# The second MoE product of three token groups as seven block products, in a kernel of linear attention followed by a MoE block

## The chip, the cores and the metric

The kernel runs on one core of a Trainium2 chip. The metric is the time of one execution on the device in microseconds (us). Five engines work side by side, each with its own queue of instructions that it takes in order: PE (TensorE, matrix products; the profile lists its weight loads apart, as PEld), DVE (VectorE), ACT (ScalarE), POOL (GpSimd) and SP, which here only issues DMAs. They wait for one another through semaphores.

## The reference

```python
def _attn_ref(q, k, v, w_phi):          # q, k, v: 8 batches, 8 heads, 576 tokens, 64 wide
    def phi(x):
        proj = np.einsum('bhsd,df->bhsf', x, w_phi)                 # 128 features
        proj = proj - np.max(np.abs(proj), axis=-1, keepdims=True)
        return np.concatenate([np.exp(proj), np.exp(-proj)], axis=-1)
    q_p, k_p = (phi(q), phi(k))
    kv = np.einsum('bhsf,bhsd->bhfd', k_p, v)
    z = np.sum(k_p, axis=2)
    num = np.einsum('bhsf,bhfd->bhsd', q_p, kv)
    den = np.einsum('bhsf,bhf->bhs', q_p, z)[..., None] + 1e-06
    return (num / den).astype(np.float32)

def _moe_ref(x, g_ln, w_ch1, w_ch2):    # x: 8 x 576 tokens, 512 wide; w_ch1 512 x 2048, w_ch2 2048 x 512
    mu = np.mean(x, axis=-1, keepdims=True)
    var = np.mean((x - mu) ** 2, axis=-1, keepdims=True)
    xn = (x - mu) / np.sqrt(var + 1e-06) * g_ln
    ch = np.maximum(xn @ w_ch1, 0.0) @ w_ch2
    return (x + ch).astype(np.float32)
```

The output of the attention, with the heads side by side, is the input x of the MoE block. Inputs and output are fp32.

## The kernel before

The eight batches are taken as four pairs. The attention of a pair is done in eight units of two heads each (32 units in all). A unit transposes its q and k (on PE in the first units, by DMA later), projects them (`pm`, `pt`), takes maxima on DVE and exponentials on ACT, scales v on POOL (`vv`), forms the kv product in two halves (`n_bank`, L945 and L951), and the numerator (`num`, L1013 and L1019). DVE scales and adds the numerator (`numc`) and POOL divides it and writes the rows of x (L1057). Nine tiles of 128 tokens belong to a pair: eight whole ones, and a mixed one that holds the last 64 tokens of both batches; half of its rows is moved between partitions by a DMA (L976).

The MoE block works on groups of NM = 4 tiles, 512 tokens: eight groups of whole tiles, numbered by pair and batch, and one group MIX of the four mixed tiles. In `moe`, a group's first product (`first`, L1246) makes 16 blocks of hidden units, each with 4 matmuls of 512 columns, and ACT or DVE apply the ReLU and write hT in bf16. The second product (`second`, L1312) makes each token tile with 16 matmuls of 512 columns; ACT or DVE scale it by the tile's 1/std, POOL or DVE add x, and SP stores it (L1221 for a whole tile; L1230, two DMAs of 64 rows, for a mixed one). The second product of a group is issued among the first products of the next one. The order of the last three groups is 6, then MIX = 7, then 8 = LAST, which holds the last four whole tiles of pair 3. The last tile of group 8 is made by `half` (L1278) in two halves of 256 columns, and DVE adds and scales in one instruction (L1286).

The order in which every engine gets its instructions is made by a planner (`Order`) ahead of the run. `add` records an operation with its engine or engines, an assumed duration, the keys that it reads and writes, and its rank; PSUM tiles are counted by `acquire` and `release`. The rank of an attention operation is its latest start plus an offset from the table OFF, by the unit's row (`stage_table`) and the kind of operation. Where PE would have nothing to do in the first 75 us of the plan, dummy products of 120 columns are put in (L1512). The DMAs of loads, of transposes and of stores go through SP's queue in the planned order.

Of the kernel before, what the change touches and what calls it, by code (L numbers as in the profile page):

```python
# [10 lines left out]
FP32 = mybir.dt.float32  # L11
# [6 lines left out]
def bcast(ap: bass.AP, dim: int, n: int) -> bass.AP:  # L18
# [7 lines left out]
RELU = -983.1  # L26
# [11 lines left out]
        "load": 291.2, "trans": -38.2, "trans.copy": 0.5, "mixed": 98.0, "mixed.max": 104.5,  # L38
        "mixed.exp": -45.3, "mixed.fold": 0.0, "k": -23.0, "k.max": 3.0, "k.em": -170.0,
        "k.exp": 48.6, "en": -19.6, "vv": 80.6, "q": -83.6, "q.max": 0.0, "q.em": -32.0,  # L40
        "tails": 0.0, "tails.exp": -33.1, "kv": -2.6, "kv.copy": 164.7, "num0": -1.6,
        "num1": -20.8, "num.dve": -35.2, "g1": 0.0, "g2": 0.0, "g3": 0.0, "put": 3.5,
# [3 lines left out]
        "load": 291.2, "trans": 67.9, "trans.copy": 77.3, "mixed": 113.2, "mixed.max": 2.5,  # L46
        "mixed.exp": 213.3, "mixed.fold": 0.0, "k": -107.2, "k.max": -82.3, "k.em": 0.0,
        "k.exp": 6.2, "en": 473.7, "vv": -103.0, "q": -117.1, "q.max": 22.6, "q.em": -113.8,
        "tails": 0.0, "tails.exp": 165.0, "kv": -37.9, "kv.copy": -50.3, "num0": 37.2,
        "num1": -11.3, "num.dve": -149.4, "g1": 0.0, "g2": 0.0, "g3": 0.0, "put": -83.2,  # L50
        "ln": -11.9, "w1": -144.2, "w2": -136.8, "ln.c": -23.8, "ln.t": -23.8,
    },
    {
        "load": 291.2, "trans": 1.5, "trans.copy": -233.5, "mixed": -82.7, "mixed.max": 122.1,
        "mixed.exp": -1.1, "mixed.fold": 0.0, "k": 0.0, "k.max": -8.9, "k.em": -29.8,
        "k.exp": 0.0, "en": 7.8, "vv": 31.7, "q": 171.9, "q.max": 0.0, "q.em": 0.0,
        "tails": -7.0, "tails.exp": 17.2, "kv": 3.1, "kv.copy": 23.8, "num0": 0.2,
        "num1": 234.6, "num.dve": 11.4, "g1": 0.0, "g2": 0.0, "g3": 0.0, "put": -23.6,
        "ln": -23.8, "w1": -144.2, "w2": 29.5, "ln.c": -23.8, "ln.t": -23.8,
    },  # L60
    {
        "load": 291.2, "trans": 88.5, "trans.copy": 90.6, "mixed": 98.6, "mixed.max": -74.3,
        "mixed.exp": -98.9, "mixed.fold": 0.0, "k": 57.3, "k.max": -34.9, "k.em": 25.5,
# [3 lines left out]
        "w2": -136.8, "ln.c": 37.5, "ln.t": 0.0,  # L67
    },
    {
        "load": 0.5, "trans": -177.0, "trans.copy": 128.5, "mixed": -1.4, "mixed.max": -3.9,  # L70
        "mixed.exp": 16.5, "mixed.fold": 0.0, "k": -79.5, "k.max": -16.8, "k.em": -20.4,
        "k.exp": -42.2, "en": -14.1, "vv": -42.3, "q": 271.6, "q.max": -32.6, "q.em": 5.9,
        "tails": -412.8, "tails.exp": -63.8, "kv": 72.7, "kv.copy": 39.3, "num0": 0.0,
        "num1": 70.0, "num.dve": -0.3, "g1": 41.9, "g2": -13.9, "g3": -5.0, "put": -25.6,
# [234 lines left out]
def kernel(  # L309
# [43 lines left out]
    NB16 = 3  # L353
# [769 lines left out]
    def token_tile(g, i):  # L1123

        pair, t = (i, MX) if g == MIX else (g // NR, g % NR * NM + i)
        if g > MIX:
            pair, t = NPAIR - 1, MX - NM + i
# [220 lines left out]
    def moe(g):  # L1348
# [3 lines left out]
        for jj in range(JC):  # L1352
            if g <= LAST:
                first(g, jj)
# [197 lines left out]
```

## Time and profile before

| | us |
|---|---|
| median of 3 runs (377.04 to 377.27) | 377.05 |
| the profiled execution, its own time | 375.46 |
| its span, first to last instruction | 373.7 |

| busy in the span | us |
|---|---|
| first products on PE (L1246, 576 matmuls) | 137.3 |
| second products on PE (L1312, 560 matmuls) | 132.5 |
| ReLU on ACT (L1256, 93 instructions) | 55.6 |
| ReLU on DVE (L1254, 51 instructions) | 35.0 |
| addition of x on POOL (L1329, 18 of the whole tiles) | 21.1 |
| last tile's result on DVE (L1286, 2 halves) | 1.0 |

The profile counts matmuls as overlapping: the shown duration of one of 512 columns, 379 ns, is its time through the pipeline, and the next one starts sooner. How fast a row of products goes is therefore read from the chain of waits or the timeline, as duration of a piece divided by its count. Busy shares are those of the engine, not of the critical path.

### The profile page before, as it was taken

The page shows a single profiled execution, that of the slowest core. Times are in us where ns is not written, and L with a number is a line of the kernel's source. Part 1 is how long each engine was busy: PE and PEld are TensorE (multiplying, and loading weights), DVE is VectorE, ACT ScalarE, POOL GpSimd, SP SyncE. Part 2 cuts the span into 40 slices and gives each one's busy share as a digit, 9 for nine tenths or more (in the row PEclk, how much of TensorE's full clock was granted, in tenths as well). Part 3 has the DMA queues.
Part 4 walks back from the last instruction along what each step waited for, and adds up shares of the span by engine and source line. Part 5 has one row for each costly group of instructions (what it writes and reads, how often), then busy time and mean ns, then how long its engine had stood idle before and what let it go on. Part 6 is the DMA issues. An engine that isn't in the chain of part 4 may idle for free.

```text
span 373.7 us, 9165 instructions
## 1 busy us (share of the span) xinstructions
PE 358.2 (96%) x3490; PEld 204.4 (55%) x3490; DVE 244.2 (65%) x517; ACT 271.0 (73%) x564; POOL 216.3 (58%) x441
## 2 busy tenths in 40 slices
PE   8968898998999999999999999999999999999995
PEld 8856784554454545555545554555455544444444
DVE  4859898986889968876797689777957740000001
ACT  4866998796979897878997899688958663643520
POOL 4597998674945867576757675775566523001211
PEclk9999999999999999999999999999999999999999
DMA  8999999989996795486539242913040043002112
GB/s 211 286 216 232 187 261 252 234 214 237 265 225 177 174 236 164 104 185 211 125 119 203 102 91 58 209 59 66 25 93 36 26 89 119 22 0 56 44 42 84
DMA packets 92587, 53.61 MB, mean 143 GB/s; under 512 B 58992, under 2 KB 87984, under 8 KB 92544
## 3 DMA queue, kind: packets, MB, share of 16 engines
q1 hardware_dynamic: 87504, 47.99, 51.1%
q0 software_dynamic: 4416, 4.49, 7.2%
q10 hardware_dynamic: 624, 0.56, 0.5%
q8 instruction: 27, 0.44, 0.5%
q14 instruction: 16, 0.13, 0.1%
HBM read 36.77 MB, written 9.44 MB: 124 GB/s over the span
## 4 chain that ended last, share of the span: by engine, by line
PE 75%; DMA 14%; DVE 7%; POOL 1%; issue 1%; SPq 0%; DVEq 0%; POOLq 0%
PE ch_ps L1312 29%; PE hT_ps L1246 29%; DMA qk<-in_q_dram 8%; DMA qkT<-b 4%; PE pm L796 3%; PE n_bank L951 3%; PE num L1013 3%; DVE m L853 2%; PE pt L805 2%; DMA qx<-in_k_dram 2%; PE n_bank L1512 1%; PE ch_ps L1278 1%; PE n_bank L945 1%; DVE numc L1037 1%; DVE hT L1254 1%
## 5 line engine op out<-in xcount | busy, mean ns | idle before, releaser
L1246 PE MATMUL hT_ps<-xT,w 128*128 128x512 bf16 x576 | 137.3, 379 | 0.5 <-DVE hT L1254 0.4
L1312 PE MATMUL ch_ps<-w,hT 128*128 128x512 bf16 x560 | 132.5, 379 | 0.0
L853 DVE TENSOR_REDUCE m<-pm 128x8 f32<-128x1024 f32 x64 | 76.7, 1215 | 11.7 <-PE pm L796 9.6
L1246 PEld LDWEIGHTS <-w 128*128 128x128 bf16 x576 | 52.1, 98 | 56.2 <-issue 2.8
L1312 PEld LDWEIGHTS <-hT 128*128 128x128 bf16 x560 | 51.6, 98 | 55.2
L1256 ACT ACTIVATE hT<-hT_ps 128x512 bf16<-128x512 f32 x93 | 55.6, 598 | 30.8 <-PE hT_ps L1246 29.4
L921 ACT ACTIVATE ea<-pt 128x1024 bf16<-128x1024 f32 x64 | 63.6, 1034 | 7.5 <-PE pt L805 7.2
L867 ACT ACTIVATE eb<-pm 128x1024 bf16<-128x1024 f32 x64 | 64.2, 1033 | 2.7 <-DVE m L853 2.7
L1057 POOL TENSOR_TENSOR x<-numc,rden 128x64 bf16<-128x64 f32 (+1 forms) x128 | 48.4, 401 | 20.8 <-DVE rden L1049 19.2
L879 POOL TENSOR_TENSOR vv<-v,em 128x512 bf16<-128x512 f32 x32 | 33.5, 1047 | 45.0 <-ACT em L858 29.3
L1286 DVE SCALAR_TENSOR_TENSOR o<-ch_ps,rstd,x 128x256 f32<-128x256 f32 x2 | 1.0, 484 | 65.8 <-PE ch_ps L1278 65.8
L1254 DVE TENSOR_SCALAR hT<-hT_ps 128x512 bf16<-128x512 f32 x51 | 35.0, 687 | 12.1 <-PE hT_ps L1246 11.7
L1329 POOL TENSOR_TENSOR o<-o,x 128x512 f32<-128x512 f32 x18 | 21.1, 1173 | 31.6 <-ACT o L1325 31.3
L1325 ACT ACTIVATE o<-ch_ps,rstd 128x512 f32<-128x512 f32 x22 | 15.1, 687 | 28.2 <-PE ch_ps L1312 28.2
L879 POOL TENSOR_TENSOR vv<-v,en 128x512 bf16<-128x512 f32 x32 | 33.4, 1043 | 1.9 <-ACT en L872 1.8
L1013 PEld LDWEIGHTS <-ea 128*128 128x128 bf16 x512 | 23.9, 97 | 10.3 <-issue 1.6
L1512 PE MATMUL n_bank<-wz 128*128 128x120 bf16 x393 | 28.4, 222 | 0.6 <-ACT KV L961 0.5
L951 PE MATMUL n_bank<-vv,eb 128*128 128x65 bf16 x512 | 26.9, 194 | 0.0
L951 PEld LDWEIGHTS <-eb 128*128 128x128 bf16 x512 | 22.3, 98 | 5.7 <-issue 1.4
L1512 PEld LDWEIGHTS <-wz 128*128 128x128 bf16 x393 | 23.9, 101 | 2.1 <-issue 1.2
L1037 DVE TENSOR_TENSOR numc<-num,em 128x390 f32<-128x390 f32 (+1 forms) x40 | 20.4, 516 | 4.3 <-PE num L1013 4.2
L1329 POOL TENSOR_TENSOR o<-o,xm 128x512 f32<-128x512 f32 x4 | 4.6, 1153 | 31.7 <-ACT o L1325 31.7
(99 smaller groups left out, 508.4 us busy)
## 6 DMA issues: line engine op xcount, KB each, us to landing
out_dram<-o SPq DMA_DIRECT2D x31, 256.0 KB, 2.8
qk<-in_k_dram SPq DMA_DIRECT2D x12, 512.0 KB, 5.8
qk<-in_q_dram SPq DMA_DIRECT2D x12, 512.0 KB, 6.9
v<-in_v_dram SPq DMA_DIRECT2D x12, 512.0 KB, 5.2
w<-in_moe_w_ch_dram POOLq DMA_DIRECT2D x8, 512.0 KB, 11.1
qk<-in_k_dram SPq DMA_DIRECT2D x8, 256.0 KB, 6.9
qk<-in_q_dram SPq DMA_DIRECT2D x7, 256.0 KB, 7.6
v<-in_v_dram SPq DMA_DIRECT2D x7, 256.0 KB, 7.9
```

What stands on the lines that cost most here:

```text
L853: nc.vector.reduce_max(out=m, in_=ps, axis=AX.X, apply_absolute_value=True)
L867: nc.scalar.activation(eb, ps, AF.Exp, scale=(1.0, -1.0)[t])
L879: nc.gpsimd.tensor_tensor(out=u["vv"][:, t, 0:MX, 0:D], in0=vb[:, hh, :].rearrange("p (c d) -> p c d", d=D), in1=bcast(e[:, 0:MX], 2, D), ...
L921: nc.scalar.activation(u["EA"][:, t, 0:1024], u["pt"], AF.Exp, scale=(1.0, -1.0)[t])
L951: nc.tensor.matmul(ps[:, t, c // 4, :], EB[:, t, c, :], vv[:, t, c, :], start=False, stop=(t == 0 and c == MX - 1), skip_group_check=True,)
L1013: nc.tensor.matmul(ps[t][:, i, :], ea(u, t, c), KV[:, t, c // 4, :], start=True, stop=True,)
L1057: nc.gpsimd.tensor_tensor(out=dst, in0=st["numc"][ps_, i : i + n, 0:D], in1=bcast(st["rden"][ps_, i : i + n], 2, D), op=ALU.mult,)
L1246: nc.tensor.matmul(st["ps"], w1_sb[:, kc, jj * P : (jj + 1) * P], xT_bufs[g % XB][:, kc::KC, :], start=(kc == 0), stop=(kc == KC - 1),)
L1254: nc.vector.tensor_relu(h_sb, st["ps"])
L1256: nc.scalar.activation(h_sb, st["ps"], AF.Relu)
L1312: nc.tensor.matmul(ch[g, i], hT[g, jj][:, i * P : (i + 1) * P], w2_sb[:, jj, :], start=(jj == 0), stop=(jj == JC - 1),)
L1512: nc.tensor.matmul(warm, wz, wz[:, 0:WN], start=False, stop=False, skip_group_check=True)
```

## The change

The last three groups (`FAST`) get another second product. For two token tiles A1 and A2 (the rows of hT, its 16 blocks of hidden units split into even and odd ones) and for w2 (rows split in the same way, columns into two halves of 256) the product is a 2 x 2 product of blocks. It is made by Strassen's scheme in Winograd's form, with seven block products instead of eight: each is 8 matmuls of 256 columns, on blocks, on four sums S of blocks of hT, or on four sums T of blocks of w2. Two pairs of tiles make up a group, so there are 14 steps of 8 matmuls; the first two products of each pair are split in halves of 4 matmuls. Three accumulators of 256 columns (`chain`) are used for a pair, and each product's partial sum is added to the output tile by DVE as it stands, seven results per pair; so a chain goes on only when the result before it has been read.

The four sums T are formed once (`weight_sums`, 8 instructions on DVE or POOL), the four sums S for each group (`token_sums`, 16 instructions on DVE, half of them after the ninth first product, half after the last). They lie in the buffers of q, k and v that the attention no longer uses. hT becomes one ring of 24 fixed slots.

The group of the mixed tiles becomes the last one (MIX = LAST = 8), and groups 6 and 7 are the whole tiles of pair 3. In the last group the second pair is stored in halves of 256 columns, each in two DMAs of 64 rows. `half` is gone. The table OFF has other numbers and one more row, for the units of pair 3.

```diff
-        "load": 291.2, "trans": -38.2, "trans.copy": 0.5, "mixed": 98.0, "mixed.max": 104.5,
+        "load": 291.2, "trans": -41.8, "trans.copy": 16.1, "mixed": -153.8, "mixed.max": 92.2,
...
-    MIX = LAST - 1
+    MIX = LAST
+    FAST = (LAST - 2, LAST - 1, LAST)
+    CP = JC // 2
+    FH = DM // 2
+    SH = CP // 2
...
+    ring = consts.tile([P, HB, RN], BF16, name="hT")
+    wide = [t.bitcast(BF16).rearrange("p a u f -> p (a u f)") for t in qk_bufs]
+    small = [t.bitcast(BF16).rearrange("p u f -> p (u f)") for t in v_bufs]
...
+    def weight_sums():
+        B11, B12 = w2_sb[:, 0::2, 0:FH], w2_sb[:, 0::2, FH:DM]
+        B21, B22 = w2_sb[:, 1::2, 0:FH], w2_sb[:, 1::2, FH:DM]
+        T1, T2, T3, T4 = T_of
+        todo = ((T1, B12, B11, ()), (T2, B22, T1, (0,)), (T3, B22, B12, ()), (T4, B21, T2, (1,)))
...
+                add(("DVE", "POOL"), (Port(0.6), 2.0), (), emit,
...
+    def token_sums(g, c):
+        for p in range(NM // 2):
...
+                out_, a, b, op = (
+                    (S1, blocks(1, 0), blocks(1, 1), ALU.add),
+                    (S2, S1, blocks(0, 0), ALU.subtract),
+                    (S3, blocks(0, 0), blocks(1, 0), ALU.subtract),
+                    (S4, blocks(0, 1), S2, ALU.subtract),
+                )[i]
+                nc.vector.tensor_tensor(out=out_, in0=a, in1=b, op=op)
...
+    def fast(g, p, i, cs):
...
+        left, right, chain, t, f, s_key, t_key = (
+            (A(t0, 0), B(0, f1), 0, t0, f1, None, None),
+            (A(t0, 1), B(1, f1), 1, t0, f1, None, None),
+            (S(1), T(1), 0, t0, f2, 1, 1),
+            (S(0), T(0), 2, t1, f2, 0, 0),
+            (S(2), T(2), 0, t1, f2, 2, 2),
+            (S(3), B(1, f2), 2, t0, f2, 3, None),
+            (A(t1, 1), T(3), 0, t1, f1, None, 3),
+        )[i]
...
+            nc.vector.scalar_tensor_tensor(
+                out=o, in0=ch[g, p][:, bank, cols : cols + FH], scalar=rstd_x[:, g, t : t + 1],
+                in1=token_tile(g, t)[2][:, f] if fresh else o, op0=ALU.mult, op1=ALU.add,
+            )
...
+        if g == LAST and p == NM // 2 - 1:
+            if not fresh or i == 6:
+                dma("SP", counts["V"], 131072, lambda: store(g, t, ch["o", g, t], f.start, f.stop),
+                    r=o_key)
...
     def moe(g):
         done = 0
+        if g == FAST[0]:
+            weight_sums()
         for jj in range(JC):
             if g <= LAST:
                 first(g, jj)
+            if g - 1 in FAST:
+                pairs_, h1, h2 = range(NM // 2), range(SH), range(SH, CP)
+                steps = [(p, i, cs) for cs in (h1, h2) for p in pairs_ for i in range(2)]
+                steps += [(p, i, range(CP)) for i in range(2, 7) for p in pairs_]
+                until = min(len(steps), -(-(jj + 1) * len(steps) // 8))
+                for step in steps[done:until]:
+                    fast(g - 1, *step)
+                done = until
+            if g in FAST and jj in (SH * 2, JC - 1):
+                token_sums(g, 0 if jj < JC - 1 else SH)
...
     def stage_table(n):
-        return min(n, H) + (n >= 2 * H)
+        return min(n, H) + (n >= 2 * H) + (n >= 3 * H)
...
-                groups = (*[g for g in groups if g < MIX], MIX, LAST)
+                groups = (*groups, MIX)
```

Over the whole program PE gets 336 matmuls of 256 columns (`fast`, L1421 of the changed file) for 176 of 512 and 32 of 256, and 402 dummy products for 393. Three places show how the change moves instructions. L numbers in the rows of the change are lines of the changed file, where everything behind the table stands lower.

The first is the end of DVE's program, in the last group. Before, DVE has nothing there but the statistics of the mixed tiles, long ahead, and the last tile's two results:

```order
L1186 BN_AGGR mv<-st 128x2
L1174 BN_STATS st<-xm 128x6
L1186 BN_AGGR mv<-st 128x2
L1191 TENSOR_SCALAR xc_137<-xm,mv 128x512
L1286 SCALAR_TENSOR_TENSOR o<-ch_ps,rstd,x 128x256 x2
```

Now the sums S of the second half of the hidden units stand there (L1375, into the old buffers qk_100, v_103 and v_105), and among them the results (L1430) of the two pairs (ch_6062 and ch_6072):

```order
L1375 TENSOR_TENSOR qk_100<-hT 128x512
L1375 TENSOR_TENSOR v_103<-hT 128x512
L1375 TENSOR_TENSOR qk_100<-qk_100,hT 128x512
L1375 TENSOR_TENSOR v_103<-v_103,hT 128x512
L1375 TENSOR_TENSOR qk_100<-hT 128x512
L1430 SCALAR_TENSOR_TENSOR o<-ch_6062,rstd,xm 128x256
L1375 TENSOR_TENSOR v_105<-hT 128x512
L1430 SCALAR_TENSOR_TENSOR o<-ch_6062,rstd,o 128x256
L1430 SCALAR_TENSOR_TENSOR o<-ch_6072,rstd,xm 128x256
L1375 TENSOR_TENSOR qk_100<-hT,qk_100 128x512
```

Five sums stand ahead of the first pair's first result, one more sum and one result ahead of the second pair's.

The second place is the end of SP's queue, with the stores of the last two groups. Before:

```order
L1221 DMA out_dram<-o 128x512 x4
L1230 DMA out_dram<-o 64x512 x8
L1221 DMA out_dram<-o 128x512 x3
L1221 DMA out_dram<-o 128x256 x2
```

And now:

```order
L1231 DMA out_dram<-o 128x512 x8
L1240 DMA out_dram<-o 64x256 x4
L1240 DMA out_dram<-o 64x512 x2
L1240 DMA out_dram<-o 64x256 x2
L1240 DMA out_dram<-o 64x512 x2
L1240 DMA out_dram<-o 64x256 x2
```

The last four tiles took five DMAs of 128 rows; they take twelve of 64 rows, of which the last ten belong to the last five pairs of DMAs.

The third place is POOL's queue in the ramp, about units 2 to 5, where POOL writes the rows of x (L1057, in the changed file L1069; `x` whole tiles, `xs` and `xm` the mixed one) and scales v (`vv`). Before, the rows of unit 3 (the rows of x in the last `128x64 x2` and the two `128x3x64`) stand behind the v of unit 4 and partly of unit 5:

```order
L1057 TENSOR_TENSOR x<-numc,rden 128x64
L1057 TENSOR_TENSOR xs<-numc,rden 64x64
L1057 TENSOR_TENSOR xm<-numc,rden 64x64
L1057 TENSOR_TENSOR x<-numc,rden 128x64 x2
L1057 TENSOR_TENSOR xs<-numc,rden 64x64
L1057 TENSOR_TENSOR x<-numc,rden 128x3x64
L879 TENSOR_TENSOR vv<-v_105,em 128x8x64
L884 CAST vv<-em 128x8
L888 TENSOR_TENSOR vv<-vx_107,em 128x130
L1057 TENSOR_TENSOR x<-numc,rden 128x3x64
```

And now:

```order
L1069 TENSOR_TENSOR x<-numc,rden 128x3x64
L588 DMA w_132<-in_moe_w_ch_dram 128x4x512
L1069 TENSOR_TENSOR x<-numc,rden 128x3x64 x3
L891 TENSOR_TENSOR vv<-v_105,em 128x8x64
L896 CAST vv<-em 128x8
L900 TENSOR_TENSOR vv<-vx_107,em 128x130
L1069 TENSOR_TENSOR x<-numc,rden 128x64 x2
L891 TENSOR_TENSOR vv<-v_105,em 128x8x64
```

Unit 3's rows of whole tiles, the last that group 0 needs, now stand ahead of unit 5's v and of three of the four halves of the v of units 4 and 5; the mixed rows `xs` and `xm` of units 2 and 3 follow behind them. On PE the transposes of group 0's tokens (L1138) stand behind nine halves of kv products where they stood behind twelve.

More of the change, by code (lines that the diff above doesn't have):

```diff
@@ new lines @@
+    {
+        "load": 7.2, "trans": 138.6, "trans.copy": 96.2, "mixed": 359.4, "mixed.max": 9.3,
+        "mixed.exp": 4.2, "mixed.fold": 0.0, "k": -33.5, "k.max": -1.4, "k.em": -15.1,
+        "k.exp": 3.5, "en": -6.3, "vv": -77.6, "q": -27.3, "q.max": -738.0, "q.em": 8.0,
+        "tails": -210.6, "tails.exp": -25.8, "kv": -17.8, "kv.copy": -18.3, "num0": 53.8,
+        "num1": 47.3, "num.dve": -78.8, "g1": 4.1, "g2": -68.2, "g3": -93.8, "put": 0.0,
+        "ln": 104.9, "w1": 193.2, "w2": 28.2, "ln.c": 8.6, "ln.t": -5.8,
@@ L1362, in moe @@
                 done += n
-        if g > LAST:
-            for c0 in range(0, DM, DM // 2):
-                for j0 in range(0, JC, 4):
-                    half(LAST, NM - 1, c0, j0, 4)
     def stage_table(n):
-        return min(n, H) + (n >= 2 * H)
+        return min(n, H) + (n >= 2 * H) + (n >= 3 * H)
     def rk(stage, n):
```

230 lines of the change are left out of this document (140 added, 90 removed), and 10 rows, old and new, of the table OFF.

## The prediction

> **What bounds the kernel now.** I read the page's first two parts, then the waits of TensorE (PE) from 100 us on, then a table by stage, then the chain that ended last.
>
> ```profile
> span 373.7 us, 9165 instructions
> PE 358.2 (96%) x3490; PEld 204.4 (55%) x3490; DVE 244.2 (65%) x517; ACT 271.0 (73%) x564; POOL 216.3 (58%) x441
> ```
> ```profile
> engine line waited for: us in total, times, longest us
> PE num L1013 <- DVE KV L959: 0.2, 1, 0.2
> ```
> ```profile
> 20.00:40.00 20.00, 15.07 (x274) 12.83 (x271) 15.66 (x37) 13.59 (x35) 17.04 (x37) 1.00 1.04 217
> 40.00:60.00 20.00, 18.37 (x321) 14.97 (x320) 18.64 (x45) 18.95 (x44) 18.10 (x41) 1.00 1.17 243
> ...
> 200.00:220.00 20.00, 20.00 (x210) 10.81 (x208) 13.04 (x25) 16.14 (x35) 13.64 (x31) 1.00 0.51 124
> 220.00:240.00 20.00, 20.00 (x181) 10.40 (x181) 18.10 (x38) 17.00 (x39) 14.09 (x29) 1.00 0.55 106
> ...
> 300.00:320.00 20.00, 20.00 (x94) 9.08 (x93) 3.52 (x11) 9.81 (x19) 4.69 (x5) 1.00 0.43 107
> 320.00:340.00 20.00, 20.00 (x95) 9.05 (x93) 0.00 (x0) 10.67 (x18) 1.15 (x1) 1.00 0.06 14
> ```
> The second block lists all that PE waited for between 100 us and the end: 0.2 us in 274. In the table (columns: stretch, length, busy us of PE, weight loads, DVE, ACT, POOL, then granted clock, DMA share, GB/s) PE has 20.00 of 20 us busy in each of these stretches, at clock 1.00; before 60 us it has not, and there the DMA engines are at 1.04 and 1.17 of their share. So there are two regimes: a ramp that loads feed, and from about 100 us a solid block of PE work whose length is simply the number of columns streamed. After 300 us nothing else is busy: DVE has 3.52 and then 0.00 of 20 us. PE work that is taken out of the block shortens the kernel one for one, unless another engine becomes late.
>
> ```profile
> 300.80 13.81 PE ch_ps L1312 x64
> 314.61 14.68 PE hT_ps L1246 x68
> ...
> 356.05 10.36 PE ch_ps L1312 x48
> 366.41 3.51 PE ch_ps L1278 x32
> 369.92 0.03 issue
> 369.94 0.48 DVE o L1286
> ```
> This is the end of the chain that ended last. A second product of one group is 64 matmuls of 512 columns in 13.81 us, so 216 ns each; the last token tile is done as 32 matmuls of 256 columns in 3.51 us, so 110 ns each. These two rows price the change.
>
> **The change, part by part.** The sum is made against the profiled execution itself, 375.46 us (its span is 373.7, and 1.8 lie around it). It lies 1.6 us under the median of the runs, 377.05, and I carry that difference over.
>
> *Products.* Three groups lose their second product: 13.81 + 13.81 + (10.36 + 3.51) = 41.49 us. Each gets 2 pairs x 7 products x 8 matmuls = 112 of 256 columns, together 336 x 3.51 / 32 = 36.86 us. That is **-4.63 us**, all of it in the solid block. The weights of such a matmul (a 128x128 load) stay hidden in the L1278 row already. A rule speaks against this: the Trainium skill (TensorE: Matmul & The Clock Gate, Back-to-back issue gap) gives pairs of weight load and matmul a sustained 81 ns at 128 columns and 131 ns at 512; a line between them gives an estimate of 98 ns at 256, and by it the change would cost 336 x 98 - 192 x 131 ns = +7.8 us. The rows differ, 216 and 110 ns, and they decide.
>
> *Filler.* In the first 75 us of the plan PE is kept warm by dummy products; the new order has 402 of them, the old 393.
> ```profile
> 1.07 3.52 PE L1512 MATMUL n_bank<-wz 128*128 128x120 bf16 x39
> 4.42 0.39 PE L633 MATMUL qkT_ps<-ident,qk 128*128 128x128 bf16 x4
> ...
> 50.67 2.05 PE L1512 MATMUL n_bank<-wz 128*128 128x120 bf16 x36
> 52.67 0.38 PE L1138 MATMUL xT_ps<-ident,xc 128*128 128x128 bf16 x4
> ```
> 36 of them lie between 50.67 and 52.67, 56 ns each, so nine are **+0.5 us**. The rest of the attention order is new too (the table of offsets), with the same products and the same bytes; I cost this at nothing, since the loads that fill the DMA engines there are the same. If that cover fails, see the rival on the ramp.
>
> *Sums of weights.* Eight sums of 1024 columns, five on POOL and three on DVE, stand about units 21 to 24, between 200 and 240 us.
> ```profile
> L708 POOL TENSOR_TENSOR b<-qk,one 128x1024 bf16<-128x1024 f32 x7 | 13.2, 1890 | 8.1 <-issue 4.9 <-DMA qkT<-b 2.2 <-PE num L1019 1.0
> ```
> At 1.9 us each POOL gets 9.5 us more, where it is busy 13.6 and 14.1 us of 20. What hides it is PE's own queue of MoE products: with every product of PE's order priced by its columns, on the line through 216 ns at 512 and 110 at 256, 10 us of work lie between unit 21's numerator and the kv product of unit 22, the first that waits behind three of these sums. Nothing on the path; without the cover at most what does not fit, some 2 us.
>
> *Sums of tokens, and results.* Per group DVE gets 16 sums of 512 bf16 elements and 14 results of 256 columns, where ACT, POOL and DVE had four results. Results are the L1286 row, 0.48 us; instructions on DVE follow each other 0.09 us before the shown end (rows below: 295.94 + 0.56, but the next starts at 296.41), so 0.4 us each.
> ```profile
> 295.94 0.56 DVE L1037 TENSOR_TENSOR numc<-num,em 128x390 f32<-128x390 f32 x1
> 296.41 0.16 DVE L1049 RECIPROCAL rden<-numc 128x3 f32<-128x3 f32 x1
> ...
> 300.88 0.67 DVE L1254 TENSOR_SCALAR hT<-hT_ps 128x512 bf16<-128x512 f32 x1
> ...
> 303.27 0.35 DVE L1191 TENSOR_SCALAR xc<-xm,mv 128x512 bf16<-128x512 bf16 x1
> ```
> No row has a sum of two bf16 tiles. Below lies the one-input bf16 operation of that size, 0.35 us, above the one that reads fp32, 0.67. I take 0.45, nearer to the bf16 row, since both operands are bf16 in SBUF; the distance between starts is then 0.36. By the Trainium skill (VectorE: DVE Perf Modes, The perf-mode tier table) a `tensor_tensor` on bf16 reaches half the rate of the one-input operations; no run here shows it yet, and it agrees with a value between the rows.
> The new wait is in the last group. PE starts its block with 32 products of hT, 3.5 us; the next product adds to columns that a result must have read first, and it takes sums. Ahead of that result DVE has five sums (the order is shown above), and the first sum needs the last ReLU, about 0.9 us after PE's last first product (0.16 of drain, 0.6 of ReLU, a semaphore). 0.9 + 5 x 0.36 + 0.4 = 3.1 us: in time. The other pair's result: + 0.36 + 2 x 0.4 = 4.3, needed at 4.4: just in time. I take **+0.1 us**. At 0.67 (0.58 apart) it is 4.2 and 5.6 against 3.5 and 5.1: 1.2 us of wait here, and about 0.2 in the first of the three groups, +1.4 us. At 0.35 it is nothing. Behind a late result stand the other pair's sums and results on DVE, and PE's products two further on.
>
> *The end.* The mixed tiles are last now; each of their stores is two DMAs of 64 rows on SP's queue, and the last pair of tiles is stored in halves.
> ```profile
> L1230 SPq DMA_DIRECT2D out_dram<-o x8: 466/562/1220, 336.6 to 353.4; - x8
> ...
> L1221 SPq DMA_DIRECT2D out_dram<-o x5: 332/338/383, 361.5 to 370.5; - x5
> ```
> Before, one DMA of 0.34 us follows the last result. A 64-row DMA took 0.47 to 0.59 us to issue (median 0.56), so a pair with the gaps takes about 1.17 us, while the last results come every 8 x 0.11 = 0.88 us. The last five pairs queue: the first is ready 3.5 us before the last result and starts at once, and the fifth ends at -3.5 + 5 x 1.17 = 2.35 us after the last result, against 0.34. That is **+2.0 us**. Nothing later hides it. If these half-size DMAs issue as fast as the 128-row ones, 0.34, a pair takes 0.76 and nothing queues; then only the second DMA is extra, +0.4. Both lie in the range; I take the row of the same 64 rows.
>
> Sum: -4.63 + 0.5 + 0.1 + 2.0 = **-2.0 us**: 373.4 profiled, **375.0** against the median. 0.2% (0.75 us) is about what a measurement of this kernel can tell from no change.
>
> **The rivals.**
> - *The stores do not queue* (+0.4 instead of +2.0): 373.4. For it: 128-row DMAs issue in 0.34. Against: the only 64-row stores took 0.56.
> - *DVE takes the sums at the fp32 rate*: -2.0 + 1.3 = 376.3. For it: many DVE rows of 512 are near 0.67. Against: the bf16 row of 0.35.
> - *The ramp gains*: the first product of group 0 stands 1.3 us of PE work earlier on PE's order (42.6 against 43.9 us of products and filler ahead of it, priced by columns as above). If its input is there, about -1.8: 373.2.
> - *The ramp loses, and the kernel is slower.* The transposes of group 0's tokens (L1138, at 52.67 us above) now stand behind nine half kv products on PE instead of twelve, with 36.3 us of products and filler ahead instead of 41.1. PE's queue is in order.
> ```profile
> 50.13 1.03 POOL L1200 TENSOR_TENSOR xc<-mv,x 128x512 bf16<-128x512 f32 x1
> ```
> Before, the last of these tokens is centred by POOL at 51.16. If the new order has it no sooner, PE stands there until 52.67 as before, but with 3.0 us less of real products done (17.8 against 20.8): -2.0 + 3.0 = 378.0. With PE as late against its work as before (52.67 - 41.1 = 11.6 us) it arrives at 47.9; the loss passes the other terms when the tokens come later than about 50. Against it: POOL and DVE do unit 3's rows and their statistics earlier in the new order, and DVE centres three tiles at 0.35 instead of ACT and POOL.
> - *A fixed charge per matmul*: were the weight load (98 ns) paid on each of the 144 added matmuls, +14.1 us, 389. The L1278 row says no; the skill's rule above is of this kind.
>
> The number of products is fixed by the order, so that the change does less than it says is no case.
>
> **How the numbers follow.** Forecast 0.55 (374.0 to 376.2), no queue of stores 0.12, ramp gains 0.06, DVE slow 0.11, ramp loses 0.15, fixed charge 0.01. Faster by over 0.2% (under 376.3): 0.53 of the forecast, 0.12, 0.06 = 0.71. Within 0.2%: DVE slow and the forecast's edge, 0.13. Slower: 0.16. The range, 372.6 to 377.8, takes in the bounds of stores and sums and the near part of a losing ramp, and leaves out about 0.15 on the high side and little on the low.
>
> **What would show it.** In the changed profile: 336 matmuls of 256 columns about 110 ns apart, a block of 112 in 12.3 us against 13.81; PE waits on DVE before a second-product line of at most 0.1 us; a sum near 0.45 us; SP's last DMAs back to back and the last one issued about 1.8 us after the last result; group 0's first product near 55 us and PE full from 100 us. Wrong would be the prediction if PE shows waits after 100 us on POOL or DVE, or if the transposes of group 0 wait.

## The result, and the profile after the change

The changed kernel took **374.82 us** in the median of 20 runs (372.86 to 378.87), the kernel before 377.05 (375.35 to 380.28) beside it. The ratio is 0.9942, with a 95% interval of 0.9917 to 0.9967: 2.2 us less, where 2.0 were forecast (375.0). A second set gave 375.22 against 377.19, ratio 0.9979 (0.9946 to 1.0013), an interval that does not exclude "no change". (The ratios are estimated from the runs in the faster of two states alone, so they need not be those of the medians.)

The spread of single runs has a cause that can be taken out. Each run lists the mean granted clock of TensorE (PE), and the 20 runs fall into groups by it: 372.9 to 373.8 us at 0.998 or 0.999, 374.6 to 376.1 at 0.994 or 0.995, 375.7 to 378.0 at 0.989 or 0.990, and one of 378.9 at 0.982. A line through them costs 3.5 us per hundredth of the clock: a share of the clock that is lost costs about the same share of the span. So below I also give a run's time less (1 - clock) x 375 us, called "at full clock": 372.7 (standard error 0.1) for the first set; 372.7 (0.4) for the second, beside 374.5 (0.2) for the kernel before on the same chip, 1.8 us less. The correction takes off a little too much, as the profiles show: the clock also falls to half some 2.6 to 5.2 us behind PE's last product, where it costs nothing. That part is 0.6 us in the profile of before, 0.4 to 1.6 in those of kernels that end like the changed one, 0.0 to 0.2 in those with two store queues, and 7.3 in `one_store`. It matters below where kernels with different ends are compared.

The profiled execution is one at clock 0.989: 376.49 us, of which the clock took 4.1, 3.4 of it while PE had work. In the 375.46 of before it took nothing from PE's work, so the two must not be set against each other as they stand. First the page of the changed kernel, and what PE waited for from 100 us on.

```profile
span 374.7 us, 9523 instructions
PE 358.0 (96%) x3627; PEld 219.6 (59%) x3627; DVE 292.1 (78%) x624; ACT 252.6 (67%) x540; POOL 213.2 (57%) x429
```
```profile
PE ch L1421 <- DVE o L1430: 0.7, 2, 0.4
PE hT_ps L1273 <- DVE hT L1281: 0.6, 1, 0.6
PE n_bank L957 <- DVE numc L1055: 0.3, 1, 0.3
```
Lines have moved: first products L1273 (L1246 before), ordinary second products L1305 (L1312), block products L1421, their results L1430 (before: L1286), token sums L1375, weight sums L1354, 64-row stores L1240 (L1230). PE has 137 matmuls more (336 - 208 + 9 fillers), and waits 1.6 us on DVE where it had waited 0.2. The table by stage (same columns as before):

```profile
20.00:40.00 20.00, 15.91 (x270) 14.08 (x267) 15.31 (x35) 15.02 (x38) 17.77 (x39) 0.91 1.16 238
40.00:60.00 20.00, 19.64 (x324) 15.39 (x322) 18.63 (x40) 17.21 (x41) 16.67 (x37) 1.00 1.13 251
60.00:80.00 20.00, 16.82 (x169) 8.78 (x168) 18.13 (x35) 13.47 (x31) 15.22 (x31) 0.91 0.90 208
80.00:100.00 20.00, 20.00 (x192) 10.90 (x191) 18.72 (x40) 17.76 (x39) 13.60 (x27) 1.00 1.07 276
...
200.00:220.00 20.00, 19.43 (x184) 10.19 (x182) 16.99 (x30) 13.87 (x29) 16.18 (x26) 1.00 0.43 105
220.00:240.00 20.00, 19.69 (x193) 10.35 (x190) 19.13 (x35) 15.85 (x35) 18.43 (x27) 1.00 0.52 123
300.00:320.00 20.00, 19.54 (x146) 13.97 (x145) 12.85 (x33) 7.56 (x16) 0.68 (x2) 1.00 0.45 113
```
PE is full from 80 us instead of 100. The clock falls to 0.91 in two stretches, some 1.7 us of full-speed work lost in each (0.09 x 20 is 1.8; finer slices give 1.7). And the solid block is no longer solid: 200 to 240 and 300 to 320 show 0.57, 0.31 and 0.46 us of idle PE, where before stood 20.00. The last block, from PE's timeline (start, length, form, idle time ahead of it):

```profile
355.53 3.66 PE L1421 MATMUL ch<-w,hT 128*128 128x256 bf16 x32
359.61 1.03 PE L1421 MATMUL ch<-qk,qk 128*128 128x256 bf16 x8 [0.43 <-DVE o L1430]
360.73 1.03 PE L1421 MATMUL ch<-qk,v 128*128 128x256 bf16 x8
361.60 1.04 PE L1421 MATMUL ch<-qk,qk 128*128 128x256 bf16 x8
362.48 1.04 PE L1421 MATMUL ch<-qk,v 128*128 128x256 bf16 x8
```
The price of a product holds: eight follow each other in 0.87 or 0.88 us, 110 ns each. But 32 of them from 355.53 on would end at 359.04, and the next starts at 359.61; its eight would end at 360.49, and the next starts at 360.73. That is 0.8 us of wait in this block, 0.9 in the first of the three (found in the same way), 0.2 in the second; with 0.7 us at 209 and 0.5 at 238 the waits behind 100 us come to 3.2 us, where the same sum gives 0.3 before.

What the ramp did is best told by work done. I add up the price of every matmul that PE has started by 100 us (216 ns at 512 columns, 110 at 256, and so on down), fillers left out, and beside it the time that lower clock took (1 - clock, summed over slices of 4 us):

| profile of | work done by 100 us | lost to the clock by then | sum |
|---|---|---|---|
| before | 64.8 us | 0.0 us | 64.8 |
| changed | 64.1 | 3.4 | 67.5 |
| changed, again | 65.5 | 1.7 | 67.2 |
| late_sums (below; the same ramp) | 67.2 | 0.0 | 67.2 |
| ramp_only (below; before with the new ramp) | 68.2 | 0.0 | 68.2 |

By the sums, the changed kernel's first profile had 2.7 us more behind it at 100 us, its filler paid, and the dips (stretches at half clock) ate that. Eight profiles with this ramp have sums from 65.5 to 67.5, mean 66.6; a ninth, of wsum_stt, lacks seven records of matmuls before 100 us and is left out. What differs between them is above all how long PE waits for q's load, 0.6 to 3.2 us. So 1.8 us is the fair figure, 0.7 to 2.7 its range. Of before there is one profile, in which PE waited 3.6 us for that load, so a part of the difference may be that execution's.

### The profile page after: what moved, and what is told of

Its sections match the earlier page's. It is cut to its first block, busy times and chain, and to the rows that moved or that the text cites. A ratio compares the mean times of both kernels' runs of the same rounds, so it can differ in the third digit from the quotient of the medians.

```text
span 374.7 us, 9523 instructions
## 1 busy us (share of the span) xinstructions
PE 358.0 (96%) x3627; PEld 219.6 (59%) x3627; DVE 292.1 (78%) x624; ACT 252.6 (67%) x540; POOL 213.2 (57%) x429
## 4 chain that ended last, share of the span: by engine, by line
PE 77%; DVE 7%; issue 2%; ACT 1%; POOL 1%; DVEq 0%
PE hT_ps L1273 31%; PE ch_ps L1305 21%; PE ch L1421 9%; PE n_bank L963 3%; PE pm L808 3%; PE num L1025 3%; PE pt L817 2%; DVE m L865 1%; PE n_bank L957 1%; DVE o L1430 1%; PE n_bank L1025 1%; PE n_bank L1031 1%; DVE qk L1354 1%; DVE numc L1049 1%; PE n_bank L1637 1%
## 5 line engine op out<-in xcount | busy, mean ns | idle before, releaser
L1273 PE MATMUL hT_ps<-xT,w 128*128 128x512 bf16 x576 | 140.0, 381 | 3.4 <-DVE hT L1281 3.0
L1305 PE MATMUL ch_ps<-w,hT 128*128 128x512 bf16 x384 | 93.2, 379 | 0.0
L1273 PEld LDWEIGHTS <-w 128*128 128x128 bf16 x576 | 52.0, 98 | 57.0 <-issue 8.1
L1069 POOL TENSOR_TENSOR x<-numc,rden 128x192 bf16<-128x192 f32 (+1 forms) x128 | 49.7, 411 | 29.7 <-DVE rden L1061 25.9
L1305 PEld LDWEIGHTS <-hT 128*128 128x128 bf16 x384 | 34.2, 98 | 34.7
L1281 DVE TENSOR_SCALAR hT<-hT_ps 128x512 bf16<-128x512 f32 x53 | 36.3, 688 | 10.4 <-PE hT_ps L1273 9.9
L1637 PEld LDWEIGHTS <-wz 128*128 128x128 bf16 x402 | 25.3, 105 | 1.6 <-issue 0.3
L1184 DVE BATCH_NORM_STATS2 st<-x 128x6 f32<-128x512 bf16 (+1 forms) x40 | 21.7, 572 | 0.3 <-POOL x L1069 0.3
L1025 PE MATMUL num<-KV,ea 128*128 128x65 bf16 x416 | 20.0, 196 | 2.0 <-ACT KV L973 2.0
L1055 DVE TENSOR_TENSOR numc<-numc,num 128x390 f32<-128x390 f32 (+1 forms) x40 | 20.4, 516 | 0.4
L808 PE MATMUL pm<-wbk,qkT 64*128 64x128 bf16 x448 | 19.9, 219 | 0.0
```

Source lines behind the costliest of these rows:

```text
L1025: nc.tensor.matmul(ps[t][:, i, :], ea(u, t, c), KV[:, t, c // 4, :], start=True, stop=True,)
L1069: nc.gpsimd.tensor_tensor(out=dst, in0=st["numc"][ps_, i : i + n, 0:D], in1=bcast(st["rden"][ps_, i : i + n], 2, D), op=ALU.mult,)
L1273: nc.tensor.matmul(st["ps"], w1_sb[:, kc, jj * P : (jj + 1) * P], xT_bufs[g % XB][:, kc::KC, :], start=(kc == 0), stop=(kc == KC - 1),)
L1281: nc.vector.tensor_relu(h_sb, st["ps"])
L1305: nc.tensor.matmul(ch[g, i], hT[g, jj][:, i * P : (i + 1) * P], w2_sb[:, jj, :], start=(jj == 0), stop=(jj == JC - 1),)
L1637: nc.tensor.matmul(warm, wz, wz[:, 0:WN], start=False, stop=False, skip_group_check=True)
```

## The experiments

Medians, ratios to the kernel before on the same chip, and times at full clock (that of one_store is some 7 us too low, since its clock fell while PE had no work):

| run | median us | ratio (95%) | at full clock |
|---|---|---|---|
| changed, again | 375.22 | 0.9979 (0.9946 to 1.0013) | 372.7 |
| third_first | 375.94 | 0.9974 (0.9935 to 1.0014) | 372.8 |
| one_store | 389.08 | 1.0334 (1.0280 to 1.0388) | 379.9 |
| offsets_only | 383.94 | 1.0193 (1.0143 to 1.0243) | 377.0 |
| two_queues | 373.06 | 0.9903 (0.9867 to 0.9939) | 371.3 |
| late_sums | 377.00 | 0.9998 (0.9960 to 1.0035) | 373.6 |
| no_weight_sums | 380.52 | 1.0123 (1.0083 to 1.0163) | 375.4 |
| ramp_only | 380.38 | 1.0100 (1.0066 to 1.0134) | 376.1 |
| cast_reduce | 372.93 | 0.9928 (0.9892 to 0.9964) | 371.5 |
| wsum_stt | 376.53 | 1.0029 (0.9996 to 1.0062) | 373.8 |
| best | 371.88 | 0.9899 (0.9866 to 0.9932) | 371.2 |
| both | **371.11** | 0.9841 (0.9794 to 0.9889) | 370.0 |

The kernel before is at 374.1 to 374.5 at full clock on the three chips.

**The changed kernel again** (no edit).

> The changed kernel once more, unaltered, as the base for the other runs. Both theories: a median near 374.8 us. The theory on record (sums and results on DVE hide behind PE, the ramp neither gains nor loses) expects PE to wait at most 0.1 us for DVE after 100 us and as much real PE work to be left at 100 us as before the change. The second theory, formed from the profile of the changed kernel, expects the waits of that profile again, at the same places and whatever the clock: 0.7 us at 209, 0.5 at 238, about 0.9 from 306 to 310 and 0.8 from 358 to 361, together about 2.9 us, and a ramp that reaches 60 us with about 1.8 us less lost than before, which the changed kernel keeps where the granted clock stays near 1.00 and loses where it falls to half for some 3.4 us behind a wait of PE.

The waits came again to a hundredth of a microsecond (0.7, 0.6 and 0.3 in the view of waits, the gaps at the same products), with a clock of 0.994 instead of 0.989: they belong to the program, not to the execution.

**Which result is waited for.** Two runs on the waits of the blocks.

```
-                steps += [(p, i, range(CP)) for i in range(2, 7) for p in pairs_]
+                steps += [(p, i, range(CP)) for i in (3, 2, 4, 5, 6) for p in pairs_]
```

> In each pair of tiles the product of S1 and T1 (new columns, needs no result read) goes ahead of the product of S2 and T2 (adds to columns that a result must have read). By the theory on record nothing waits there and the time stays: 374.8, within 0.2. By the second theory the waits on DVE in the last and the first block go, 0.9 + 0.8 us: about 373.1, a block of 112 products in 12.3 us from its first product to its last one's end.

Missed: nothing moved. From the timelines of the changed kernel (first fence) and of this run (the other two):

```profile
357.76 0.42 DVE L1375 TENSOR_TENSOR qk<-hT 128x512 bf16<-128x512 bf16 x1
358.35 0.48 DVE L1430 SCALAR_TENSOR_TENSOR o<-ch,rstd,xm 128x256 f32<-128x256 f32 x1 [0.17 <-PE ch L1421]
358.75 0.42 DVE L1375 TENSOR_TENSOR v<-hT 128x512 bf16<-128x512 bf16 x1
359.08 0.48 DVE L1430 SCALAR_TENSOR_TENSOR o<-ch,rstd,o 128x256 f32<-128x256 f32 x1
```
```profile
361.13 0.48 DVE L1430 SCALAR_TENSOR_TENSOR o<-ch,rstd,o 128x256 f32<-128x256 f32 x1
```
```profile
361.66 1.03 PE L1421 MATMUL ch<-qk,qk 128*128 128x256 bf16 x8 [0.43 <-DVE o L1430]
```
In the changed kernel PE starts at 359.61, 0.05 after the end of the *second* result of the pair (359.08 + 0.48), not after the first (358.83). In this run another product stands there, one that writes columns nobody has read, and it too starts 0.05 after the second result (361.61). Its columns lie in the bank that the second result reads, so this run alone could not tell bank from tile; the changed kernel's product lies in the other bank, the first result's, and waits as long. The two banks of a pair are one tile in the program, and a product waits for every earlier reader of the tile, in whichever bank.

The next run keeps PE's order and clears DVE's: no sums between the first and the second result.

```
-                token_sums(g, 0 if jj < JC - 1 else SH)
+                token_sums(g, 0 if jj < JC - 1 else SH, (0, 1, 3, 2) if jj < JC - 1 else (0, 1))
...
+                    if k == 8:
+                        token_sums(g - 1, SH, (3, 2), [("o half", g - 1, 2, 0)])
                     fast(g - 1, *step)
```

> The order of PE's products is that of the changed kernel; on DVE the sums S3 and S4 of the second half come behind the first four results of a group, and the first result of a pair is followed at once by its second. The theory from the last run: PE's next product waits for the second result of its pair (the one that reads the other bank of the same tile), and sums that stand ahead of it make it late. Then the waits of 0.59 + 0.25 us in the last block fall to 0.2 or less, and the 0.4 + 0.25 + 0.31 in the first block by at least half: 0.9 to 1.5 us faster at the same clock. Rival: the waits come from the sums that the next product reads (S2) and stay as they are.

A miss on the whole. The last block's waits fell from 0.84 to 0.58 us, less than expected. The first block's rose from 0.95 to 1.5:

```profile
304.09 1.04 PE L1422 MATMUL ch<-qk,v 128*128 128x256 bf16 x8
306.10 0.27 PE L1422 MATMUL ch<-qk,qk 128*128 128x256 bf16 x1 [0.97 <-DVE o L1431]
```
```profile
305.17 0.48 DVE L1431 SCALAR_TENSOR_TENSOR o<-ch,rstd,o 128x256 f32<-128x256 f32 x1 [1.01 <-PE ch L1422]
305.56 0.48 DVE L1431 SCALAR_TENSOR_TENSOR o<-ch,rstd,x 128x256 f32<-128x256 f32 x1
```
The second result of the other pair now stands behind that pair's next product in the program. It waits 1.01 us for it (304.09 + 1.04), though it reads the other bank, and PE waits 0.97 in turn. The rule of whole tiles holds in both directions; the sums alone are not the wait. The whole was not 0.9 to 1.5 us faster but 0.8 slower at full clock (error 0.3), of which the waits explain 0.3; the rest stays open.

**The end.** Two ways to shorten SP's queue.

```
-            for bi in range(2):
-                nc.sync.dma_start(
-                    out=out[b0 + bi, 4 * P : S, c0:c1], in_=o[bi * 64 : (bi + 1) * 64, c0:c1]
-                )
+            nc.sync.dma_start(
+                out=bass.AP(
+                    tensor=out.tensor, offset=out.offset + (b0 * S + 4 * P) * DM + c0,
+                    ap=[[S * DM, 2], [DM, 64], [1, c1 - c0]],
+                ),
+                in_=o[:, c0:c1],
+            )
```

> Each mixed tile, or half of one, is stored by one DMA of 2 x 64 rows instead of two of 64. If the end is late because 64-row DMAs queue on SP, at 0.64 us each from start to start, whatever their bytes, the queue goes: the last DMA is issued within 0.1 us of the last result instead of 2.2 behind it, and the kernel is 1.8 to 2.2 us faster, about 372.8. Rival: the issue time follows the rows or runs of a DMA, so that one of 2 x 64 rows takes about 1.2 us and the queue stays: 374.8.

A clear miss, 12 us slower than before. SP's timeline shows the last store's issue, and the table by stage what the transfers did:

```profile
372.65 5.88 SPq L1239 DMA_DIRECT2D out_dram<-o  x1
```
```profile
372.00:390.00 18.00, 0.00 (x0) 0.00 (x0) 0.00 (x0) 0.00 (x0) 0.00 (x0) 0.59 0.12 44
```
Four of the six stores are issued in 0.51 to 0.67 us, like a 64-row one, the last two in 2.4 and 5.88. Only 0.12 of the 16 DMA engines is busy until the end: two engines. The Trainium skill (DMA: Bandwidth & Descriptors, Why a DMA increments its semaphore by 16 and not by 1) says that a DMA runs on the largest number of engines, up to 16, that divides the slowest dimension on both sides; the slowest dimension of this one is 2, and the trace agrees.

```
-                nc.sync.dma_start(
+                (nc.sync, nc.scalar)[bi].dma_start(
```

> Of the two 64-row stores of a mixed tile the second goes to ACT's queue, idle there. If each issue takes about 0.64 us of its own queue, from start to start, and the queues do not hinder each other, a pair takes 0.64 against results every 0.88 and nothing queues: last issue within 0.2 us of the last result instead of 2.2 behind it, from the last result to the end of the span 3.5 us instead of 5.4, the kernel 1.7 to 1.9 us faster at the same clock. Rival: what limits is shared by both queues (the writing of the bytes): then the last issue comes earlier and the end does not.

As expected at the end. SP's queue at the end of the changed kernel, then SP and ACT here:

```profile
367.61 0.60 SPq L1240 DMA_DIRECT2D out_dram<-o  x1
368.30 0.55 SPq L1240 DMA_DIRECT2D out_dram<-o  x1
370.87 1.19 SPq L1240 DMA_DIRECT2D out_dram<-o  x2
```
```profile
370.30 0.56 SPq L1240 DMA_DIRECT2D out_dram<-o  x1
```
```profile
370.30 0.50 ACTq L1240 DMA_DIRECT2D out_dram<-o  x1
```
In the changed kernel the last result ends at 369.27 and the last pair is issued from 370.87 to 372.06; here the last result ends at 370.27 and both stores start at 370.30. From the last result to the end of the span it is 3.6 us instead of 5.4, 1.8 less. At full clock the kernel is 1.4 us faster (error 0.3), under the 1.7 to 1.9 expected; there the changed kernel is flattered by the 0.4 us or more that the correction takes off behind its last product and not off this kernel's.

**The weight sums.**

```
-        if g == FAST[0]:
-            weight_sums()
...
         def T(n):
-            return lambda c: T_of[n][:, c, :]
+            return B((0, 1, 0, 1)[n], f2)
```

> Leaves out the eight sums of weights; the products read plain blocks of the weights instead, as many and as wide. On record these sums cost nothing, hidden behind 10 us of PE's queue: the time would stay. From the changed kernel's profile they cost the two waits at 209 (0.7 us, behind a sum on DVE that took 2.58 us beside one on POOL) and 238 (0.5 us): 1.0 to 1.3 us faster at the same clock, and PE without a wait between 200 and 240 us.

```profile
200.00:220.00 20.00, 20.00 (x202) 10.69 (x195) 16.42 (x30) 13.70 (x31) 14.61 (x28) 1.00 0.42 109
220.00:240.00 20.00, 20.00 (x171) 10.26 (x169) 15.06 (x31) 13.26 (x31) 10.65 (x20) 1.00 0.46 110
```
This kernel leaves the sums out and multiplies by plain blocks. In its stage it behaves as the second reading said: PE full where it had 0.57 and 0.31 us idle. The kernel as a whole is slower, not 1.0 to 1.3 us faster, since the order that is planned without these sums puts one first product where it waits 4.7 us from 313 on, and the clock then stands at half for 3.4 us. So only the stage can be read, and not as one price: its order is another too. The wait at 209 stands behind a weight sum. The one at 238 stands behind another instruction of DVE, a centring that takes 0.35 us elsewhere, beside a cast on POOL:

```profile
236.75 1.56 DVE L1201 TENSOR_SCALAR xc<-x,mv 128x512 bf16<-128x512 bf16 x1
```
```profile
236.26 1.89 POOL L720 TENSOR_TENSOR b<-qk,one 128x1024 bf16<-128x1024 f32 x1
```
Whether the weight sums bring those two together is not shown. Their own price is the 0.7 us at 209.

```
-                    eng.tensor_tensor(out=out_[:, cs], in0=a[:, cs], in1=b[:, cs], op=ALU.subtract)
+                    if engine == "DVE":
+                        nc.vector.scalar_tensor_tensor(
+                            out=out_[:, cs], in0=a[:, cs], scalar=one, in1=b[:, cs],
+                            op0=ALU.mult, op1=ALU.subtract,
+                        )
...
```

> Same order on every engine; the three weight sums on DVE are made by an instruction with a scalar factor of one. Theory: the sum at 206.6 took 2.58 us since it started beside one on POOL (2.12 us), where a lone one took 0.75; the other form runs beside POOL in about 1.2 us, so that PE's wait of 0.7 us at 209 goes: 0.5 to 0.8 us faster at the same clock. Whether the 0.5 us at 238 goes too is open. Rival: the form makes no difference, the sum takes 2.5 us again.

Missed, on the wrong side. DVE and POOL of the changed kernel, then DVE and POOL here:

```profile
206.57 2.58 DVE L1354 TENSOR_TENSOR qk<-w,qk 128x1024 bf16<-128x1024 bf16 x1
```
```profile
206.49 2.12 POOL L1354 TENSOR_TENSOR qk<-w,qk 128x1024 bf16<-128x1024 bf16 x1
```
```profile
204.88 3.11 DVE L1354 SCALAR_TENSOR_TENSOR qk<-w,one,qk 128x1024 bf16<-128x1024 bf16 x1
```
```profile
204.79 2.12 POOL L1359 TENSOR_TENSOR qk<-w,qk 128x1024 bf16<-128x1024 bf16 x1
```
The sum ends 0.54 us behind the POOL instruction in the form that takes 0.75 us alone, and 1.08 behind it in the form that takes 1.29: in both 0.21 less than its time alone. So in either form it waited until POOL was about done and then took its time. Both forms read two operands from SBUF. The waits at 209 and 238 grew to 1.3 us each, the second because the centring of above now starts with POOL's cast and takes 2.06 us.

**The ramp.**

```
 before's OFF, rows 0 to 7 (units 0 to 7) replaced by the new rows       (ramp_only)
 before's OFF and row choice replaced by the new ones altogether        (offsets_only)
```

> The kernel before with the new table of offsets alone: the order of the attention work changes, the MoE products and the stores stay as before. The theory on record gave the new order nothing but some half a microsecond of filler: 377.1 to 377.6. The second theory has the ramp gain 1.8 us or more: 374 to 375.3, with more real PE work done at 60 and at 100 us than before.

> The kernel before with the first eight rows of the new table (units 0 to 7, up to about 75 us), all else as before. If the new order of the ramp is worth what the two ledgers say (2.6 us less lost at 100 us, once the time at half clock is taken out), this kernel is 2 to 3 us faster than before at the same clock. On record it was costed at nothing but half a microsecond of filler: 0 to 0.5 us slower. Third: its gain is lost again behind 100 us, since the old order of units 8 to 31 does not follow it.

Both kernels were slower than before, 383.9 and 380.4 us. The views of waits, from 100 us on, of offsets_only (largest two) and of ramp_only:

```profile
PE pm L804 <- DVE m L861: 2.2, 1, 2.2
PE n_bank L953 <- POOL vv L896: 1.1, 1, 1.1
```
```profile
PE num L1013 <- DVE numc L1043: 1.6, 1, 1.6
PE pm L796 <- DVE mv L1186: 0.8, 1, 0.8
PE num L1013 <- DVE m L853: 0.5, 1, 0.5
```
ramp_only reaches 100 us with 3.4 us more work done than before (68.2 against 64.8), and loses it between 165 and 176 us, where the old order of the later units meets the new ramp: its third expectation. The three waits take 2.9 us, and the clock at half from 168.9 to 175.7 takes up to 3.4 more. offsets_only loses between 282 and 296, around the last heads: 5.2 us of waits, and up to 5.1 by the clock at half from 285.7 to 295.9. So the gain of the new ramp by 100 us does not hang on the block products, but in these two kernels the order behind it, set for other work, gave more than that away.

**The stall in the new ramp.** DVE, POOL and PE of the changed kernel, and its table by stage around it:

```profile
57.92 4.13 DVE L716 CAST b<-qk 128x1024 bf16<-128x1024 f32 x1
61.97 0.68 DVE L1281 TENSOR_SCALAR hT<-hT_ps 128x512 bf16<-128x512 f32 x1
```
```profile
58.11 1.89 POOL L720 TENSOR_TENSOR b<-qk,one 128x1024 bf16<-128x1024 f32 x1
...
61.10 0.40 POOL L900 TENSOR_TENSOR vv<-vx,em 128x130 bf16<-128x130 f32 x1
```
```profile
62.70 1.80 PE L1273 MATMUL hT_ps<-xT,w 128*128 128x512 bf16 x4 [2.38 <-DVE hT L1281]
```
```profile
60.00:62.00 2.00, 0.32 (x2) 0.04 (x1) 2.00 (x2) 1.73 (x2) 1.92 (x4) 1.00 0.79 231
62.00:64.00 2.00, 1.30 (x4) 0.54 (x4) 2.00 (x6) 0.00 (x0) 1.84 (x5) 0.70 0.32 67
64.00:66.00 2.00, 2.00 (x21) 1.08 (x20) 1.40 (x4) 0.00 (x0) 0.47 (x2) 0.50 1.07 201
66.00:68.00 2.00, 2.00 (x17) 1.00 (x16) 1.55 (x4) 1.94 (x3) 0.30 (x2) 0.95 1.00 189
```
A cast that takes 0.7 us elsewhere stands 4.13 us beside POOL's chain, a ReLU waits behind it, PE waits 2.4 us for that, and then the clock is at half for 1.2 + 2.0 + 0.2 = 3.4 us, 1.7 us more.

```
-            if engine == "DVE" and in_.shape[2] == D:
+            if engine == "DVE":
                 nc.vector.tensor_reduce(
```

> Same order on every engine; the five 1024-column casts on DVE are made by a reduction over one element each. In the changed kernel four of them take 0.7 us and the one at 57.9 takes 4.13 us, ending after a run of POOL instructions; PE then waits 2.4 us for a ReLU behind it, and in five of six profiles of kernels with this ramp the granted clock falls to half for some 3.4 us behind that wait. Theory: the cast cannot run beside POOL's instructions, the reduction can: about 1.2 us each, the wait at 60 us shrinks to under 0.5, the dip behind it goes in most executions, and the kernel is 2 to 4 us faster in the median (371 to 373). Rival: DVE is held up by something else there (its buffer, or the data): the reduction takes as long, and nothing changes.

```profile
55.19 1.21 DVE L711 TENSOR_REDUCE b<-qk 128x1024 bf16<-128x1024 f32 x1
```
As expected at the place: 1.21 us beside POOL, no wait of PE there, no dip behind it. The median is 372.93, where the changed kernel's two sets had 374.82 and 375.22: 1.9 and 2.3 us less, the low end of the 2 to 4 expected. At full clock it is 1.2 us (error 0.3), half of the wait that went; what took the rest is not shown. The Trainium skill (SBUF — State Buffer, Who interferes with whom) has the rule for both runs: DVE shares a port with POOL for casts in its fast modes and for instructions with two SBUF inputs, an instruction with one input outside those modes does not. The traces agree: 4.13 and 2.58 and 3.11 against 1.21 us.

**Together.**

> Both of the above and the stores on two queues (1.4 us faster when alone, at the same clock). If the three are independent: 2.4 + 0.6 + 1.4 us and the dip that goes: a median of 369 to 370.5. If a later wait takes the place of the one at 60 us, 371 to 372.

> The stores on two queues and the casts by reduction together, the weight sums as in the changed kernel. Taken as independent (1.4 us and about 2.2 us off the median of 375.0): 370.5 to 371.7, some 5 us under the kernel before. Rival: the weight sums in the form with a factor did not matter to the last run but one, and this one lands where that did, at 371.9.

`best` (casts by reduction, stores on two queues, weight sums with a factor) took 371.88, where its last alternative had put it; it has the waits of wsum_stt, 1.3 + 1.3 us at 206 and 235. `both` leaves the weight sums as they were and took **371.11 us**, 5.8 less than the kernel before beside it (376.88): the first two edits add up within their error.

## Why the prediction came out, step by step

The sum was right, -2.0 forecast and -1.8 (at full clock) to -2.2 (medians) measured, but in part by luck: two errors cancel, waits that I had not priced, and a ramp that I had costed at nothing. By the sign that I had named myself the prediction was wrong: it was to fail if PE showed waits after 100 us on POOL or DVE, and the view has 1.6 us of them on DVE.

- *Products, -4.63*: right. 110 ns each, 336 of them; no trace of a charge per weight load.
- *Filler, +0.5*: the count is right, 402 records, and they still follow each other in 57 ns (34 in 1.95 us at 50.00).
- *"The rest of the attention order ... I cost this at nothing, since the loads that fill the DMA engines there are the same"*: wrong, by the largest amount. The DMA engines were as full (1.16 and 1.13 against 1.04 and 1.17), yet PE had 2.7 us more done by 100 us, clock aside. The transposes of group 0 came at 46.00 instead of 52.67, its first product at 52.68 instead of 55.31 ("near 55"), and PE was full from 80 instead of 100. The rival "the ramp gains" (1.8 us for that part, chance 0.06) had the right size and went the right way; "the ramp loses" (0.15) was wrong, the tokens were there in time. The cover I named covers less than I thought: of the 11.5 us that the view of waits lists for PE in the first 100 us before, the loads ended only 4.1, and the new order removed others, the two largest among them:

```profile
PE pt L805 <- DVE numc L1043: 1.5, 1, 1.5
PE n_bank L945 <- POOL vv L888: 1.1, 2, 0.6
```
The listed waits of the changed kernel come to 8.7 us there, though one of 2.4 is new.
- *Sums of weights, nothing*: wrong, by the 0.7 us at 209. The cover I named (PE's queue ahead of the next kv product) held for POOL: PE waits for no sum there. What failed is that the three sums on DVE got no price at all: one of them stands 2.58 us beside one on POOL, and a ReLU behind it is late. The 0.5 us at 238 is a like collision of other work, a centring beside a cast.
- *Sums of tokens and results*: the sizes were right, 0.42 us shown and 0.33 apart (0.45 and 0.36), 0.48 for a result; the rival of the fp32 rate falls. *The wait, +0.1*, was wrong: 0.8 in the last block, 0.9 and 0.2 in the others. The step that failed is "a result must have read first": it takes both results of the pair. My 3.1 us to the end of the first was nearly right (3.30 from 355.53), but a sum and the second result come on top (4.03), against 3.5 needed.
- *The end, +2.0*: right. Last DMA issued 2.2 us after the last result (1.8 forecast; a pair took 1.28 us of the queue, not 1.17), last result to end of span 5.4 us against 3.2 before: +2.2. That the halves issue as slowly as whole tiles held too: 0.55 and 0.60 us.

For the two profiles: -4.6 (products) + 1.2 (waits at 209 and 238) + 1.9 (waits in the blocks) - 0.3 (the one of before) + 2.2 (the end) - 2.7 (the ramp with its filler) = -2.3, where 376.49 - 3.4 against 375.46 makes -2.4. With the ramp's mean of 1.8 it is -1.4, somewhat less than the -1.8 at full clock; 0.4 us lie within the error of that mean and of the one profile of before.

## What to carry to other kernels

When work is taken out of a full engine, look in the same sum at what the engines beside it now get: here DVE went from 65 to 78% busy, and where it was late PE waited. Price an instruction of VectorE (DVE) beside what GpSimd (POOL) does at that moment, and where the two overlap choose a form that does not wait: here the reduction over one element did not, while a cast and a centring with one tile as input did, like the sums of two. A store that is split in two costs an issue each; two idle queues hide what one cannot.

## What the runs showed of the hardware

- After a wait of 2.4 us at 60 us PE's clock was at half for about 3.4 us, in seven of nine profiles of kernels with that wait; the five without it show no dip there. In six profiles such a dip also stands at 35 to 38 us, in the first one behind two waits of 1.1 and 1.2. A dip costs 1.7 us, and single runs of one kernel fall into groups about that far apart by their clock; that the groups differ by the number of dips is inferred, since the unprofiled runs give only the mean clock.
- Several waits close together in the solid block had longer stretches at half clock with them: 6.8 us in ramp_only (three waits within 6 us), 10.2 in offsets_only (five within 9). One wait of 4.5 us, in no_weight_sums, had 3.4.
- Back to back, the second 64-row store of a pair starts 0.60 us after the first and the next pair 0.68 or 0.69 after that, whether a store moves 128 KB or 64; SP's and ACT's queues issue side by side.
- A DVE cast of 1024 columns waited not for one POOL instruction but for a chain of four without a gap: 4.13 us for 0.68. A sum of two tiles waited for one of 2.12 us, in either of two forms.
